# Up 2 of a two-layer feed-forward kernel: one of three token groups as seven products for eight, and every engine's order written down

## The chip, the core and the metric

The program runs on one core of one Trainium2 chip: TensorE (PE) multiplies, ScalarE (ACT), VectorE (DVE) and GpSimd (POOL) work on vectors, SyncE (SP) issues all transfers. The metric is the device time of one execution in microseconds; lower is better.

## The reference, cut to what matters

```python
attn_out = _attn_ref(**attn_kwargs)              # attention in chunks of 32, with 8 memory keys
x = attn_out.transpose(0, 2, 1, 3).reshape(B * S, H * D)       # 3072 tokens x 512
h = x @ w_in;  g = s * relu(h) ** 2 + b;  x = g @ w_out        # 512 -> 2048 -> 512
h = x @ w_in2; g = h - tanh(h);           return g @ w_out2    # 512 -> 2048 -> 512
```

All inputs are float32.

## The kernel before, in words

Five stages follow each other: attention mixed with **Up 1** (x @ w_in), **Down 1** (g @ w_out), **Up 2** (x @ w_in2 and the curve h - tanh h) and **Down 2** (g @ w_out2). In every matrix product each operand is split into a rounded "high" half and the rest, its "low" half, and the helper `three` (L123) adds high*high, low-weight*high and high-weight*low into a bank of PSUM. So a product of a 128x128 block of weights with 512 tokens is three matmuls of 128x128 by 128x512. Weights come from DRAM as 64-bit floats (`raw`) and are made float32 in four steps: `scaled` on ScalarE, `shifted`, `signed` and `filled` on VectorE. Then ScalarE copies the high half and another engine subtracts it for the low half.

The 3072 tokens are three groups (g = 0, 1, 2; NG = 3) of 1024. A product of 2 x 2 blocks can be had from seven products of sums of blocks in place of eight (P1 to P7; Strassen's scheme in Winograd's form). Down 1 and Down 2 do this before and after the change: the outer loop goes over the seven products in `ORDER` (P1, P6, P5, P7, P3, P2, P4), the inner over the three groups, each in four **entries** of 12 matmuls. So a Down stage is 7 x 3 x 4 x 12 = 1008 matmuls. For each entry `split` makes the high half (ScalarE) and the low half (VectorE) of a loaded `part` in a ring of three buffers, two entries ahead of TensorE; the third matmul of an entry is the first that reads the low half. `final` adds a finished bank to the running sums. Ready sums of g's blocks are formed at the end of each Up block by `combine` (four subtractions of 512 columns) and stored to DRAM.

Up 2 before takes the weights in eight blocks n of 1024 columns a row; each block meets the three groups with all eight products: 4 x 12 = 48 matmuls for a group, 8 x 3 x 48 = 1152 in all. Two banks are filled (24 matmuls), ScalarE takes the tanh (L794), VectorE subtracts (L795), and after two such halves GpSimd runs `combine` (L796).

The order of all engines is written by hand (`tc.manual_schedule()`) from the start to the last entry of the first product of Down 1. From there only TensorE's order is by hand (`region.enter_context(tc.manual_schedule(engines={nc.tensor.engine}))`) and a scheduler orders the others. Each engine runs its instructions in its queue's order. An instruction that waits holds what is behind it.

Of the kernel before, what the change touches and what calls it, by code (L numbers as in the profile page):

```python
# [48 lines left out]
"""  # L49

# [8 lines left out]
def tile_chunk_attention_two_ffn(  # L59
# [50 lines left out]
    def bank(k):  # L110
        return pb[:, 512 * k:512 * (k + 1)]
# [11 lines left out]
    def three(acc, whi, wlo, xhi, xlo, first, last):  # L123
        nc.tensor.matmul(acc, lhsT=whi, rhs=xhi, start=first, stop=False)  # L124
        nc.tensor.matmul(acc, lhsT=wlo, rhs=xhi, start=False, stop=False)  # L125
        nc.tensor.matmul(acc, lhsT=whi, rhs=xlo, start=False, stop=last)  # L126
# [22 lines left out]
    def to_f32(z, raw):  # L149
# [201 lines left out]
    def make_pair(raw, z_place, place, key, n, lo_pool=True):  # L351
        z = new(z_place, 1024, F32, "z")
        to_f32(z, raw)
        w = new(place, 2048, F32R, "w")
        hi, lo = w[:, 0:1024], w[:, 1024:2048]
        nc.scalar.activation(out=hi, in_=z, func=AF.Copy)
        (nc.gpsimd if lo_pool else nc.vector).tensor_tensor(out=lo, in0=z, in1=hi.bitcast(F32), op=ALU.subtract)
        wi[key, n] = tuple(t.rearrange("p (i c m) -> p i c m", i=2, c=KD) for t in (hi, lo))

# [71 lines left out]
    class Down:  # L431
# [55 lines left out]
        def sums(self, p, half, eng):  # L487

            z = lambda k: self.z[k, half]
            name = ORDER[p]  # L490

            def combo(i, x, y, op):
                t = new(self.smap[i][half], 1024, F32, f"s{i}")
                eng.tensor_tensor(out=t, in0=x, in1=y, op=op)
                self.st[i, half] = t
                return t

            if name == "P1":
                src = z("A11")
            elif name == "P6":  # L500
                s1 = combo(0, z("A21"), z("A22"), ALU.add)
                src = combo(1, s1, z("A11"), ALU.subtract)
            elif name == "P5":
                src = self.st[0, half]
            elif name == "P7":
                src = combo(0, z("A11"), z("A21"), ALU.subtract)
            elif name == "P3":
                src = self.st[1, half]
                eng.tensor_tensor(out=src, in0=z("A12"), in1=src, op=ALU.subtract)  # L509
            else:  # L510
# [46 lines left out]
        def run(self, between):  # L557
# [49 lines left out]

    def final1(name, g, ps):
        a = lambda k: sums1.at(k, g)

        def last_sum(k, x, op):
# [50 lines left out]
    region = ctx.enter_context(ExitStack())  # L662
    region.enter_context(tc.manual_schedule())
# [13 lines left out]
    for j in range(2, NBLK):  # L677
        last = j == NBLK - 1
        for t in range(16):
# [15 lines left out]
            if last and t in (4, 10):  # L695
                down1.weights(0, t // 8, nc.vector)
# [81 lines left out]

    for n in range(8):
        for g in range(NG):  # L780
            at_ = NG * n + g
            oa, ob = (
                new(C_OT[at_ % 2][h], 4 * NB, F32, ("oa", "ob")[h]).rearrange("p (s t) -> p s t", s=4)
                for h in range(2)
            )
            wh, wl = wi[2, n]
            for i in range(2):
                ps = bank2((2 * at_ + i + 1) % 4)
                for col, half in enumerate((1, 0)):
                    for c in range(KD):  # L790
                        xh, xl = x2_of(c, half, g)
                        three(ps[:, col, 0:NB], wh[:, i, c, :], wl[:, i, c, :], xh, xl, c == 0, c == KD - 1)
                r = new(C_R[i], 2 * NB, F32, "r2").rearrange("p (m t) -> p m t", m=2)
                nc.scalar.activation(out=r, in_=ps[:, :, 0:NB], func=AF.Tanh)  # L794
                nc.vector.tensor_tensor(out=oa[:, 2 * i:2 * i + 2], in0=ps[:, :, 0:NB], in1=r, op=ALU.subtract)  # L795
            combine(oa, ob, nc.gpsimd)  # L796
            nc.sync.dma_start(out=o2[g][:, n, 0:3], in_=oa[:, 1:4])
            nc.sync.dma_start(out=o2[g][:, n, 3:7], in_=ob)
            if g == 0 and n + 1 < 8:
                w2_load(n + 1)  # L800
            if g == 1 and n + 1 < 8:
                w2_make(n + 1)
            if g == 0 and 1 <= n <= 4:
                thunks.extend(down2.load_quadrant(C_RAW[1 + i]) for i in range(2))
            if g in (1, 2) and thunks:
                thunks.pop(0)()
            if n == 7 and g in (1, 2):
                down2.weights(0, g - 1)
                down2.load_to(g - 1)
    down2.run(lambda p, k: None)  # L810
# [71 lines left out]
```

## Time and profile before

| what | value |
| --- | --- |
| median of 3 runs | 1081.1 us (1080.97 to 1082.42) |
| profiled execution | 1080.99 us, span 1079.2 us |
| TensorE busy | 1060.4 us (98%), mean granted clock 0.996 |
| VectorE, ScalarE, GpSimd busy | 711.6, 486.6, 265.1 us |
| TensorE's share of the chain that ended last | 91% |

The span runs from the first to the last instruction; the profiled execution took 1.8 us more than its span. A matmul's busy time (0.39 us) overlaps the next one's, so TensorE's pace is read from starts. Idle time of an engine other than TensorE costs nothing by itself.

### The profile page before, as it was taken

To read this page: it belongs to the slowest core of one execution; us is meant where nothing else is said; L and a number is where in the kernel's file an instruction comes from. 1 tells how busy PE (TensorE), PEld (TensorE's weight loads), DVE (VectorE), ACT (ScalarE), POOL (GpSimd) and SP (SyncE) were. 2 spreads that over 40 slices of the span, in tenths; PEclk is the share of its full clock that TensorE was granted. 3 is DMA by queue.
4 is the path that set the end of the run, shared out by engine and by line. 5 is a ranking of instruction groups with operands and counts; after the bars stand their busy time and mean duration, and the time that the engine had idled before them with its cause. 6 is when DMAs were issued, how large, how long until landed. Compare 5 with 4: busy or idle time off the path is not lost.

```text
span 1079.2 us, 15211 instructions
## 1 busy us (share of the span) xinstructions
PE 1060.4 (98%) x6072; PEld 876.1 (81%) x6072; DVE 711.6 (66%) x742; ACT 486.6 (45%) x863; POOL 265.1 (25%) x164
## 2 busy tenths in 40 slices
PE   6999999999999999999999999999999999999998
PEld 5878888888888878888888888888888888888886
DVE  7997667777768895578788894332322665566654
ACT  7673665555423554455554342222222454444432
POOL 1000000000000161100100587655567941001100
PEclk8999999999999999999999999999999999999999
DMA  9764768666448856555565756545546865566751
GB/s 319 262 254 167 264 237 318 246 249 222 179 183 317 299 189 201 194 193 198 194 236 176 305 197 265 215 166 205 214 171 228 312 234 195 195 234 234 252 196 59
DMA packets 71687, 242.16 MB, mean 224 GB/s; under 512 B 5312, under 2 KB 5312, under 8 KB 61376
## 3 DMA queue, kind: packets, MB, share of 16 engines
q1 hardware_dynamic: 71616, 241.19, 62.3%
q8 instruction: 47, 0.77, 0.3%
q14 instruction: 24, 0.20, 0.0%
HBM read 146.80 MB, written 94.37 MB: 223 GB/s over the span
## 4 chain that ended last, share of the span: by engine, by line
PE 91%; DVE 5%; ACT 2%; DMA 2%; issue 1%; DVEq 0%; ACTq 0%; SPq 0%
PE pb L124 29%; PE pb L126 29%; PE pb L125 29%; PE pb L298 2%; PE pb L276 2%; PE pb L236 1%; DMA raw<-in_wi_dram 1%; ACT sm L260 1%; DVE ringhringl L535 1%; DVE ob L423 1%; DVE oa L408 0%; DVE z L145 0%; DVE w L378 0%; DVE nmx L254 0%; DMA qk<-in_qk_dram 0%
## 5 line engine op out<-in xcount | busy, mean ns | idle before, releaser
L126 PE MATMUL pb<-ringhringl,whl 128*128 128x512 f32 x560 | 218.3, 390 | 0.9 <-DVE ringhringl L535 0.9
L124 PE MATMUL pb<-ringhringl,whl 128*128 128x512 f32 x560 | 217.9, 389 | 0.0
L125 PE MATMUL pb<-ringhringl,whl 128*128 128x512 f32 x560 | 217.9, 389 | 0.0
L540 DVE TENSOR_TENSOR ringhringl<-part,ringhringl 128x1024 fp32r<-128x1024 f32 x92 | 128.5, 1397 | 84.7 <-ACT ringhringl L539 84.7
L539 ACT ACTIVATE ringhringl<-part 128x1024 fp32r<-128x1024 f32 x92 | 97.7, 1061 | 135.6 <-PE pb L126 123.2
L124 PE MATMUL pb<-xh,w 128*128 128x512 f32 (+1 forms) x392 | 153.5, 392 | 0.4 <-DVE oa L408 0.3
L126 PE MATMUL pb<-xl,w 128*128 128x512 f32 (+1 forms) x392 | 151.2, 386 | 0.6 <-DVE xl L320 0.6
L125 PE MATMUL pb<-xh,w 128*128 128x512 f32 (+1 forms) x392 | 151.1, 386 | 0.1
L795 DVE TENSOR_TENSOR oa<-pb,r 128x1024 f32<-128x1024 f32 x48 | 58.5, 1220 | 109.7 <-ACT r L794 104.6
L126 PEld LDWEIGHTS pb<-ringhringl,whl 128*128 128x128 f32 x560 | 105.1, 188 | 24.9 <-DVE ringhringl L535 2.9
L125 PEld LDWEIGHTS pb<-ringhringl,whl 128*128 128x128 f32 x560 | 105.1, 188 | 21.8
L124 PEld LDWEIGHTS pb<-ringhringl,whl 128*128 128x128 f32 x560 | 105.1, 188 | 21.7
L794 ACT ACTIVATE r<-pb 128x1024 f32<-128x1024 f32 x48 | 49.1, 1025 | 124.8 <-PE pb L126 124.3
L509 POOL TENSOR_TENSOR s<-zq,s 128x1024 f32<-128x1024 f32 x4 | 12.4, 3093 | 374.8 <-DVE whl L521 374.7
L398 ACT ACTIVATE r<-pb 128x512 f32<-128x512 f32 x96 | 55.9, 592 | 99.1 <-PE pb L126 84.8
L535 DVE SCALAR_TENSOR_TENSOR ringhringl<-part,b_c,ringhringl 128x1024 fp32r<-128x1024 f32 x48 | 76.7, 1613 | 22.2 <-ACT ringhringl L534 21.9
L408 DVE SCALAR_TENSOR_TENSOR oa<-pb,s_c,r 128x512 f32<-128x512 f32 x96 | 70.0, 745 | 29.0 <-ACT r L398 29.0
L124 PEld LDWEIGHTS pb<-xh,w 128*128 128x128 f32 x392 | 73.6, 188 | 17.5 <-DVE oa L408 1.7
L124 PE MATMUL pb<-x2hx2l,w 128*128 128x512 f32 x224 | 87.1, 389 | 0.0
L125 PE MATMUL pb<-x2hx2l,w 128*128 128x512 f32 x224 | 87.1, 389 | 0.0
L126 PE MATMUL pb<-x2hx2l,w 128*128 128x512 f32 x224 | 87.1, 389 | 0.0
L126 PEld LDWEIGHTS pb<-xl,w 128*128 128x128 f32 x392 | 73.6, 188 | 15.7 <-DVE xl L320 0.8
(108 smaller groups left out, 1811.2 us busy)
## 6 DMA issues: line engine op xcount, KB each, us to landing
o<-ob SPq DMA_DIRECT2D x48, 1024.0 KB, 4.7
part<-o SPq DMA_DIRECT2D x84, 512.0 KB, 4.6
part<-o SPq DMA_DIRECT2D x42, 1024.0 KB, 5.0
o<-oa SPq DMA_DIRECT2D x48, 768.0 KB, 3.5
raw<-in_wi_dram SPq DMA_DIRECT2D x16, 1024.0 KB, 6.4
raw<-in_wo_dram SPq DMA_DIRECT2D x16, 1024.0 KB, 7.0
qk<-in_qk_dram SPq DMA_DIRECT2D x24, 640.0 KB, 7.7
v<-in_vw_dram SPq DMA_DIRECT2D x24, 384.0 KB, 8.1
```

The costliest lines, as they stand in the source:

```text
L124: nc.tensor.matmul(acc, lhsT=whi, rhs=xhi, start=first, stop=False)
L125: nc.tensor.matmul(acc, lhsT=wlo, rhs=xhi, start=False, stop=False)
L126: nc.tensor.matmul(acc, lhsT=whi, rhs=xlo, start=False, stop=last)
L276: nc.tensor.transpose(out=bank(2 + g)[0:KE, P * r:P * (r + 1)], in_=sm[:, 4 * g + r, :], identity=ident)
L298: nc.tensor.matmul(value_bank(u)[64 * g:64 * g + 64, c0:c0 + QE], lhsT=tv[0:KE, e, 2 * r + g, :], rhs=pt[0:KE, 4 * g + r, QE * e:QE * (e + ...
L398: nc.scalar.activation(out=r, in_=up_ps[j, t], func=AF.Relu)
L408: nc.vector.scalar_tensor_tensor(out=oab[j, q][0][:, 2 * i:2 * i + 2, k, :], in0=ps2, scalar=s_c[:, 0:1], in1=r2, op0=ALU.mult, op1=ALU.mult,)
L535: nc.vector.scalar_tensor_tensor(out=xl, in0=src, scalar=self.bias, in1=xh.bitcast(F32), op0=ALU.add, op1=ALU.subtract)
L539: nc.scalar.activation(out=xh, in_=src, func=AF.Copy)
L540: nc.vector.tensor_tensor(out=xl, in0=src, in1=xh.bitcast(F32), op=ALU.subtract)
L794: nc.scalar.activation(out=r, in_=ps[:, :, 0:NB], func=AF.Tanh)
L795: nc.vector.tensor_tensor(out=oa[:, 2 * i:2 * i + 2], in0=ps[:, :, 0:NB], in1=r, op=ALU.subtract)
```

## The change

Up 2 computes the third group (g = 2) with the seven products; groups 0 and 1 stay as they were. The products are accumulated in three single banks (0, 1, 2): P1, P6, P5 and P3 follow each other in bank 0, and ScalarE copies the bank (`keep`) after P1, P6 and P5, before the next product is added to it. P7 and P4 share bank 1, P2 has bank 2. Token sums T1 to T4 are made at the end of Down 1 (`b_t3`, `b_t1`, `b_t2`) and split in block 0 of Up 2 (`t_split`), weight sums in every block (`w2_sums`, `w2_split`). All subtractions that GpSimd did go to VectorE. The order of all engines is by hand to the program's end; in the Down stages the steps that make the next product's weights stand at places given by a table `WEIGHTS`. Buffers are placed anew. Of the diff (buffer places, and what repeats, left out):

```diff
+WEIGHTS = {
+    (0, 1): [("sums", 1, 0)], (0, 2): [("high", 1, 0)], (0, 4): [("low", 1, 0)],
...
-    C_RAW, C_Z, C_W = ("E0", "E8", "E10"), "Z5", ("E1", "E2")
+    C_RAW, C_Z, C_W = "E0", "Z5", ("E1", "E2")
...
+    D_RAW = ("E0", "E1")
...
-        def weights(self, p, half, eng=nc.gpsimd):
-            self.sums(p, half, eng)
+        def weights(self, p, half):
+            self.sums(p, half)
             self.high(p, half)
-            self.low(p, half, eng)
...
-                elif p + 1 < 7 and k in (5, 9):
-                    self.weights(p + 1, (k - 5) // 4)
+                for step, q, half in WEIGHTS.get((p, k), ()):
+                    getattr(self, step)(q, half)
                 between(p, k)
...
-        if p == 0 and k == 4 * NG - 1:
-            region.close()
-            region.enter_context(tc.manual_schedule(engines={nc.tensor.engine}))
...
+        if p == 6 and k < 3:
+            (lambda: (w2_load(0), b_t3()), b_t1, b_t2)[k]()
+        if p == 6 and 4 <= k < 4 + len(w2_steps):
+            w2_steps[k - 4](0)
...
+    def end_out(n, g):
+        oa, ob = outs.pop((n, g))
+        combine(oa, ob, nc.vector)
+        nc.sync.dma_start(out=o2[g][:, n, 0:3], in_=oa[:, 1:4])
+        nc.sync.dma_start(out=o2[g][:, n, 3:7], in_=ob)
...
+        strassen("P1")
+        copy(1)
+        strassen("P7")
+        strassen("P6")
+        copy(2)
+        yield
+        strassen("P5")
+        copy(3)
+        strassen("P2")
+        add(2, 3, 1)
+        strassen("P3")
+        add(1, 1, 2)
+        strassen("P4")
+        yield
+        curve(0, bank(0))
+        curve(1, oa[:, 1])
+        curve(2, oa[:, 2])
+        add(3, 2, 1)
+        curve(3, oa[:, 3])
+        yield
+        end_out(n, g)
...
     for n in range(8):
...
+        for col in range(2):
+            plain_column(n, 1, 0, col)
+        if last:
+            quads[3]()
...
+        else:
+            w2_steps[0](n + 1)
+        plain_end(n, 1, 0)
+        if last:
+            quads[4]()
+            fetch(6, 1)
...
+            down2.load_to(0)
+        else:
+            for step in w2_steps[1:]:
+                step(n + 1)
...
+        plain_column(n, 1, 1, 0)
+        group = quad(n)
+        next(group)
+        plain_column(n, 1, 1, 1)
+        plain_end(n, 1, 1)
+        next(group)
+        end_out(n, 1)
+    down2.load_to(1)
+    down2.split(0)
+    down2.split(1)
+    next(group)
```

`w2_steps` holds six steps for the next block's weights: `scaled` with `shifted`; `signed`; `filled`; high half (ScalarE); low half; the four weight sums of 256 columns. `curve` is a tanh on ScalarE and a subtraction on VectorE, `add` one sum on VectorE. In a block TensorE's order is: both columns of half (0,0), of (0,1) and of (1,0), 24 matmuls each; a column of (1,1), 12; P1, P7, P6, 6 each; the other column of (1,1), 12; P5, P2, P3, P4, 6 each: 138 matmuls.

ScalarE in Up 2, block 1, from the conversion of block 2's weights on. L144 is `scaled`, L877 the tanh of a plain half, L749 the high half of the next block's weights, L900 the copies of bank 0 (`keep`), L909 the curves.

```order
L144 ACTIVATE z<-raw 128x1024
L877 ACTIVATE r_5382<-pb 128x1024
L749 ACTIVATE w<-z 128x1024
L900 ACTIVATE keep<-pb 128x512 x2
L877 ACTIVATE r_5444<-pb 128x1024
L900 ACTIVATE keep_5411<-pb 128x512
```

The rows of the kernel before at such a place (L794 the tanh, L356 the high half, L131 `scaled`):

```order
L794 ACTIVATE r_5248<-pb 128x1024
L356 ACTIVATE w<-z 128x1024
L131 ACTIVATE z<-raw 128x1024
L794 ACTIVATE r_5283<-pb 128x1024
L516 ACTIVATE whl<-zq 128x1024
```

The copies of bank 0 are new, and two of them stand behind the high half of the next block's weights, which waits for VectorE's `filled` of the same block; TensorE's P6 waits for the first copy, P5 for the second.

VectorE in Down 1, product P7, second group: before the change, L616 finishes Q, L624 adds to U, L540 is the low half of a split, L621 the low half of Q for Up 2.

```order
L616 TENSOR_TENSOR q<-sumV,pb 128x1024
L624 TENSOR_TENSOR sumU<-sumU,pb 128x1024
L540 TENSOR_TENSOR ringhringl<-part,ringhringl 128x1024
L621 TENSOR_TENSOR x2hx2l<-q,x2hx2l 128x1024
L540 TENSOR_TENSOR ringhringl<-part,ringhringl 128x1024
```

And with the change (L630, L639, L646 and L547 are the same four):

```order
L630 TENSOR_TENSOR q<-sumV,pb 128x1024
L639 TENSOR_TENSOR x2hx2l<-q,x2hx2l 128x1024
L646 TENSOR_TENSOR sumU<-sumU,pb 128x1024
L547 TENSOR_TENSOR ringhringl<-part,ringhringl 128x1024 x2
```

Q's low half, which needs ScalarE's high half of the same Q, has moved ahead of the next split.

VectorE at the border of Up 2 and Down 2, with the change, from the last `combine` (L430) of group 1 on. L547 is a split of Down 2, L910 a curve's subtraction, L903 an `add`, L501 the weight sums of P6.

```order
L430 TENSOR_TENSOR ob<-ob,oa 128x512
L547 TENSOR_TENSOR ringhringl<-part,ringhringl 128x1024 x2
L910 TENSOR_TENSOR oa<-pb,r_6779 128x512
L910 TENSOR_TENSOR oa<-oa,r_6779 128x512
L910 TENSOR_TENSOR oa<-oa,r_6784 128x512
L903 TENSOR_TENSOR oa<-keep,pb 128x512
L910 TENSOR_TENSOR oa<-oa,r_6784 128x512
L547 TENSOR_TENSOR ringhringl<-part,ringhringl 128x1024
L430 TENSOR_TENSOR ob<-oa 128x512
L430 TENSOR_TENSOR ob<-oa,ob 128x512
L430 TENSOR_TENSOR ob<-oa 128x512
L430 TENSOR_TENSOR ob<-ob,oa 128x512
```

Behind them stand a split (L547), the two sums (L501), two splits and one weight conversion. Before the change VectorE's rows at this border are:

```order
L540 TENSOR_TENSOR ringhringl<-part,ringhringl 128x1024
L795 TENSOR_TENSOR oa<-pb,r_6602 128x1024
L795 TENSOR_TENSOR oa<-pb,r_6642 128x1024
L795 TENSOR_TENSOR oa<-pb,r_6669 128x1024
L540 TENSOR_TENSOR ringl<-part,ringh 128x1024
L540 TENSOR_TENSOR ringhringl<-part,ringhringl 128x1024 x2
```

The sums of g and of the weights, which were GpSimd's, now stand between the splits, and the first two splits stand behind the last `combine` of group 1.

## Rows read from the trace of the kernel before

**Rows 1.** Page, part 1: each engine's busy time and share of the span.

```profile
PE 1060.4 (98%) x6072; PEld 876.1 (81%) x6072; DVE 711.6 (66%) x742; ACT 486.6 (45%) x863; POOL 265.1 (25%) x164
```

**Rows 2.** Busy time by stretch: Down 1, Up 2, Down 2; (x) counts starts.

```profile
353.55:584.38 230.83, 229.89 (x1009) 188.83 (x1008) 178.86 (x134) 122.37 (x115) 45.26 (x16) 1.00 0.60 203
584.38:845.50 261.12, 261.12 (x1153) 216.29 (x1152) 119.05 (x91) 74.24 (x73) 167.47 (x106) 1.00 0.58 223
845.50:1074.04 228.54, 228.54 (x1009) 188.96 (x1007) 137.97 (x102) 100.09 (x96) 49.67 (x19) 1.00 0.61 212
```

**Rows 3.** Timeline of VectorE in Down 1: start, us, line, tiles, count.

```profile
379.20 1.28 DVE L535 SCALAR_TENSOR_TENSOR ringhringl<-part,b_c,ringhringl 128x1024 fp32r<-128x1024 f32 x1 [0.97 <-ACT ringhringl L534]
...
381.53 19.18 DVE L535 SCALAR_TENSOR_TENSOR ringhringl<-part,b_c,ringhringl 128x1024 fp32r<-128x1024 f32 x7
```

**Rows 4.** Timeline of GpSimd in the same stretch of Down 1.

```profile
381.76 3.31 POOL L509 TENSOR_TENSOR s<-zq,s 128x1024 f32<-128x1024 f32 x1 [8.21 <-DVE whl L521]
...
395.16 3.27 POOL L494 TENSOR_TENSOR s<-zq 128x1024 f32<-128x1024 f32 x1
```

**Rows 5.** Timeline of Down 2: TensorE, VectorE and ScalarE around a bank's last product.

```profile
1030.29 0.39 PE L126 MATMUL pb<-ringhringl,whl 128*128 128x512 f32 x1
...
1030.72 1.06 ACT L539 ACTIVATE ringhringl<-part 128x1024 fp32r<-128x1024 f32 x1 [1.89 <-PE pb L126]
...
1030.72 1.22 DVE L753 TENSOR_TENSOR o<-sumX,pb 128x1024 f32<-128x1024 f32 x1 [0.63 <-PE pb L126]
```

**Rows 6.** Timeline of ScalarE in Up 2: a curve.

```profile
682.50 1.03 ACT L794 ACTIVATE r<-pb 128x1024 f32<-128x1024 f32 x1 [4.41 <-PE pb L126]
```

**Rows 7.** Timeline of VectorE in Up 2: the subtraction behind that curve.

```profile
683.56 1.22 DVE L795 TENSOR_TENSOR oa<-pb,r 128x1024 f32<-128x1024 f32 x1 [4.16 <-ACT r L794]
```

**Rows 8.** Timeline of VectorE in Up 1: one weight conversion.

```profile
171.00 0.68 DVE L135 TENSOR_SCALAR zq<-zq 128x1024 int32<-128x1024 int32 x1
...
171.72 1.22 DVE L139 SCALAR_TENSOR_TENSOR zq<-raw,zq 128x1024 int32<-128x1024 int32 x1
...
172.97 1.22 DVE L145 SCALAR_TENSOR_TENSOR zq<-raw,zq 128x1024 int32<-128x1024 int32 x1
```

**Rows 9.** Timeline of VectorE in Up 1: four sums and what follows.

```profile
204.08 0.68 DVE L423 TENSOR_TENSOR ob<-oa 128x512 f32<-128x512 f32 x1
...
206.61 0.75 DVE L408 SCALAR_TENSOR_TENSOR oa<-pb,s_c,r 128x512 f32<-128x512 f32 x1
```

**Rows 10.** Timeline of VectorE in Up 2: the end of a conversion.

```profile
640.90 1.21 DVE L145 SCALAR_TENSOR_TENSOR zq<-raw,zq 128x1024 int32<-128x1024 int32 x1
```

**Rows 11.** Timeline of ScalarE in Up 2: `scaled`, then a copy that waits for VectorE.

```profile
629.60 1.14 ACT L131 ACTIVATE zq<-raw 128x1024 f32<-128x1024 f32 x1
...
642.20 1.06 ACT L516 ACTIVATE whl<-zq 128x1024 fp32r<-128x1024 f32 x1 [10.55 <-DVE zq L145]
...
643.17 1.92 ACT L794 ACTIVATE r<-pb 128x1024 f32<-128x1024 f32 x2
```

**Rows 12.** Page, part 5: reads of one 512-column bank by ScalarE.

```profile
L398 ACT ACTIVATE r<-pb 128x512 f32<-128x512 f32 x96 | 55.9, 592 | 99.1 <-PE pb L126 84.8
```

**Rows 13.** Timeline of VectorE in Down 1: the end of a P7 product.

```profile
475.61 1.22 DVE L616 TENSOR_TENSOR q<-sumV,pb 128x1024 f32<-128x1024 f32 x1 [0.40 <-PE pb L126]
...
476.75 1.22 DVE L624 TENSOR_TENSOR sumU<-sumU,pb 128x1024 f32<-128x1024 f32 x1
...
477.88 1.22 DVE L540 TENSOR_TENSOR ringhringl<-part,ringhringl 128x1024 fp32r<-128x1024 f32 x1
...
479.02 1.22 DVE L621 TENSOR_TENSOR x2hx2l<-q,x2hx2l 128x1024 fp32r<-128x1024 f32 x1
```

**Rows 14.** Timeline of GpSimd at the border of Up 2 and Down 2.

```profile
847.89 2.40 POOL L509 TENSOR_TENSOR s<-zq,s 128x1024 f32<-128x1024 f32 x1
```

**Rows 15.** Loads of part (835 to 900 us) and raw (584 to 840 us).

```profile
DMA to landing us min/median/max: 4.7/6.4/7.6
...
DMA to landing us min/median/max: 4.8/6.0/7.4
```

More of the change, by code (lines that the diff above doesn't have):

```diff
@@ L121, in tile_chunk_attention_two_ffn, with three @@
     b_c = const.tile([P, 1], F32, name="b_c")
[L123 to L126, printed above, removed]
+    def three(acc, whi, wlo, xhi, xlo, first, last, more=False):
+        nc.tensor.matmul(acc, lhsT=whi, rhs=xhi, start=first, stop=False, skip_group_check=more)
+        nc.tensor.matmul(acc, lhsT=wlo, rhs=xhi, start=False, stop=False, skip_group_check=more)
+        nc.tensor.matmul(acc, lhsT=whi, rhs=xlo, start=False, stop=last, skip_group_check=more)
     def scaled(z, raw):
@@ L349, in load_raw @@
         return raw
[L351 to L358, printed above, removed]
     raws, w1_z, w1_w = {}, {}, {}
@@ L695, in tile_chunk_attention_two_ffn @@
             if last and t in (4, 10):
-                down1.weights(0, t // 8, nc.vector)
+                down1.weights(0, t // 8)
             if last and t in (4, 10, 11):
@@ L777, in tile_chunk_attention_two_ffn @@
     )
-    for n in range(8):
[L780 to L809, printed above, removed]
@@ new lines, in tile_chunk_attention_two_ffn, with fetch @@
+    quads = {}
+    def fetch(k, place=0):
+        quads[k] = down2.load_quadrant(D_RAW[place])
+    group = None
+    for n in range(8):
+        last = n == 7
+        before = group
+        begin_out(n, 0)
+        for col in range(2):
+            plain_column(n, 0, 0, col)
+        if before is not None:
+            next(before)
+        if n in (2, 4, 6):
+            quads[n // 2 - 1]()
+        if not last:
+            w2_load(n + 1)
+        else:
+            fetch(3, 0)
+            fetch(4, 1)
+        plain_end(n, 0, 0)
+        if before is not None:
+            next(before)
+        if n == 0:
+            t_split("T3")
+            t_split("T2")
+        w2_split(n)
+        for col in range(2):
+            plain_column(n, 0, 1, col)
+        plain_end(n, 0, 1)
+        end_out(n, 0)
+        if n == 0:
+            t_split("T1")
+            t_split("T4")
+        begin_out(n, 1)
+        for col in range(2):
+            plain_column(n, 1, 0, col)
+        if last:
+            quads[3]()
+            down2.sums(0, 0)
+            down2.high(0, 0)
+            down2.low(0, 0)
+            fetch(5, 0)
+        else:
[4 more added lines that the diff above has]
+            fetch(6, 1)
+            down2.sums(0, 1)
+            down2.high(0, 1)
+            down2.low(0, 1)
+            down2.load_to(0)
+        else:
+            for step in w2_steps[1:]:
+                step(n + 1)
+            if n in (1, 3, 5):
+                fetch(n // 2)
+        plain_column(n, 1, 1, 0)
[5 more added lines that the diff above has]
+        end_out(n, 1)
@@ L813, in _up_layout, with between2 @@
+    down2.load_to(1)
+    down2.split(0)
+    down2.split(1)
+    next(group)
+    def between2(p, k):
+        if p == 0 and k == 0:
+            next(group)
+        if p == 0 and k == 3:
+            quads[5]()
+            fetch(7, 0)
+        if p == 1 and k == 6:
+            quads[6]()
+        if p == 1 and k == 9:
+            quads[7]()
+    down2.run(between2)
 def _up_layout(w):
```

173 lines of the change are left out of this document (140 added, 33 removed).

## The prediction

> **What bounds it now.** The first view is the page's busy shares: TensorE is busy for 98% of the span [rows 1]. So time comes only from matmuls left out and from places where TensorE stops. The windows of the three stages show where these are [rows 2]. Up 2 starts 1152 matmuls in 261.12 us and is busy for all of it, so one matmul costs 261.12/1152 = 0.2267 us at a granted clock of 1.00: 2.72 us an entry or column of 12, 1.36 a product of 6, 5.44 a half of 24. Down 2 takes 228.54 us for 1008 matmuls, which is 1008 x 0.2267 = 228.5: no stop. Down 1 takes 230.83 us, 2.3 to 2.4 more. The timelines say where that goes: VectorE's split takes 1.28 us alone and 19.18/7 = 2.74 us [rows 3] while GpSimd sums weights between 381.76 and 398.4 us [rows 4]. Nothing else stops TensorE from Down 1 on, so a vector engine matters only where its chain is longer than the matmuls ahead of the one that waits for it.
>
> The pieces of such chains. ScalarE or VectorE starts 0.43 us after the start of a bank's last matmul [rows 5], so 0.43 - 0.23 = 0.20 us after that matmul's slot. A tanh takes 1.03 us [rows 6], and VectorE's subtraction starts 0.03 us behind it [rows 7]. Behind one another, VectorE's 1024-column instructions start 1.14 us apart [rows 13], a conversion's `shifted` and `signed` take 0.72 and 1.25 us to the next start, `filled` 1.22 us [rows 8], four 512-column sums 2.53 us [rows 9]. A ScalarE copy starts 0.09 us after VectorE's `filled` has ended [rows 10, 11], the next instruction 0.97 us later, `scaled` takes 1.14 us [rows 11], and reading one bank 0.59 us [rows 12]. From there to a waiting matmul I take 0.08 us, an estimate by the 0.03 and 0.09 above.
>
> **The change part by part.**
>
> *Matmuls.* Up 2 has 138 a block in place of 144: 8 x 6 x 0.2267 = **-10.9**.
>
> *GpSimd leaves Down 1's head.* Without its sums beside VectorE the splits should take 1.28 us again: **-2.4**, the whole loss of that stage.
>
> *P6's wait in Up 2.* P6 needs ScalarE's copy of bank 0 after P1. In ScalarE's queue that copy stands behind the high half of the next block's weights, which waits for VectorE's `filled`, and `filled` stands behind the subtraction of half (1,0). From that half's end: 0.20 + tanh 1.03 + 0.03 + subtraction 1.14 + `signed` 1.25 + `filled` 1.22 + 0.09 + high half 0.97 + copy 0.59 + 0.08 = 6.60 us. Meanwhile TensorE has a column, P1 and P7, 24 matmuls or 5.44 us. That is 1.16 us of stop, in blocks 1 to 6: **+7.0**. What is queued behind the high half is the first copy, and TensorE itself waits for it; P5's copy follows freely. Block 7 makes no next weights of this stage, and its high halves wait on nothing of VectorE: 0. The rest of the seven products (VectorE's `add`s, the curves one block later) has at least the 24 matmuls of a half to hide in: 0; if that cover were gone, a 512-column sum is 0.68 us [rows 9].
>
> *Block 0* also splits the token sums. From the end of half (0,1): 0.20 + 1.03 + 0.03, then VectorE without a gap: subtraction 1.14, `combine` 2.53, two low halves 2.28, `shifted` 0.72, subtraction of half (1,0) 1.14, `signed` 1.25, `filled` 1.22; then 0.09 + 0.97 + 0.59 + 0.08. Together 13.26 us against 24 + 24 matmuls, 10.88: **+2.4**.
>
> *Down 1, product P7.* Q's low half now stands before the splits. Before, Q, U, split and Q's low half started 1.14 us apart with nothing waiting between [rows 13]. Now, from a bank's end: 0.20 + Q 1.22 + 0.09 + ScalarE's copy 1.06 + 0.03 + Q's low half 1.14 + U 1.14 + split 1.23 + 0.08 = 6.19 us, and the third matmul of the entry that needs this split comes after two entries and two matmuls, 5.89: 0.30 for each group, **+0.9**. If ScalarE's copy is hidden, it is 0.
>
> *Down 1, product P4, entry 10.* ScalarE and VectorE wait for each other twice on the way from g = 0's sum to the split of entry 10: a sum, four ScalarE instructions, six of VectorE (the conversion's `signed` and `filled` among them), three of ScalarE, a low half. With the pieces above that ends 17.7 us after the bank, and six entries and two matmuls are 16.8: **+1.0**.
>
> *Down 2's head.* Call the end of Up 2's last product T. VectorE's last `combine` of group 1 stands behind an `add` that waits for P2, whose bank is ready at T - 2.72 + 0.20 = T - 2.52. `add` 0.60 and `combine` 2.53 bring it to T + 0.61, split 0 (1.23) to T + 1.84; the third matmul of entry 0 is due at T + 0.45, so at least 1.5 us of stop. Split 0's load was issued by SP behind the load of weights that waits for the conversion before it, about T - 6.5. It lands 4.7 to 7.6 us later [rows 15], then copy, 0.03 and split: 1.5 to 3.1 us of stop, of which I take 2.0 (near the median, 6.4, the `combine` and the load both bind). Then VectorE has 14.5 us in one queue from T + 0.7 on: two splits, four curves and an `add` with their wait for P4's tanh, a split, `combine`, a split, two weight sums of 1024 columns, the split of entry 4. That ends near T + 15.2, and entry 4's third matmul is due at T + 10.88 + 0.45: 3.9 to 4.6 us late in all. ScalarE's high half of the sum, its `scaled` and the next conversion on VectorE follow, with 3.1 us for the conversion's three steps by [rows 8]; entries 6 and 8 are then 6.4 to 6.8 late, with a late load up to 9. I take **+7.0**, range +6.5 to +9. Before, the sums at this place were GpSimd's [rows 14] and no entry waited [rows 2].
>
> The Trainium skill's page "SBUF — State Buffer", section "The DMA setup-cost knee", gives a transfer about 2 us and its bytes at 436 GB/s, an estimate of 4.4 us for a megabyte. The trace differs: 4.7 us at the least and 6.4 in the median for such a load [rows 15]. By the page's figure the load would never bind and the stop at entry 0 were 1.5 us, the sum 1085.5.
>
> *Sum*, from the profiled execution of 1080.99 us (its median of runs is 1081.1, the same within 0.1): 1081.0 - 10.9 - 2.4 + 7.0 + 2.4 + 0.9 + 1.0 + 7.0 = **1086.0 us**.
>
> **Rivals.**
>
> *A, the copy is not held up: faster.* The wait of P6 decides at 5.44 us: if the chain is 1.2 us shorter, as it is if the scheduler of the queues lets ScalarE take the copy of bank 0 ahead of the waiting high half, the +7.0 and +2.4 go: 1086.0 - 9.4 = **1076.6**. For it: ScalarE is busy 74 of 261 us in Up 2 [rows 2], so it has room. Against: at 642.20 us its copy sat 10.55 us waiting for VectorE's `filled`, and two tanhs started only behind it, at 643.17 [rows 11].
>
> The Trainium skill's page "TensorE: Matmul & The Clock Gate", in the specification table at its head, calls the queues of ScalarE and VectorE strictly first in, first out. By that A cannot come about, and the trace's tanhs agree.
>
> *B, Down 2's head is hidden*: 1086.0 - 7.0 = **1079.0**, about the time of before. It needs the first splits ready before T, so the `combine` of group 1 ahead of the `add` that waits. For it: the ring has three buffers, and the first load is issued in block 7. Against: the order of VectorE's rows.
>
> *C, the weights come late in Up 2.* In blocks 2, 4 and 6 the buffer of raw weights first serves a conversion for Down 2, so that the load of the next block's weights starts only some 8 us into the block. Landing at +7.4 it is just in time (15.4 us, then `scaled` 1.14 before 16.5); each us over that adds one to each of three blocks. For it: the longest landing of such loads is 7.4, and 7.6 for parts [rows 15]. With +2.4 to +5.4, and Down 2's parts 1.5 late, it gives **1090 to 1092**. Against: the median is 6.0.
>
> **How the numbers follow.** Forecast 0.58, A 0.13, B 0.17, C 0.12. A measurement tells about 0.2%, 2.2 us, from no change: 1078.9 to 1083.3. The forecast's own bounds: the P7 and P4 terms 0 to 1.9, Down 2's head 6.5 to 9, the 0.20 and 0.08 of each P6 chain +-0.2 x 7: 1082.7 to 1089.4; nearly all of it is slower, 0.55, with 0.03 the same. A is faster; B lies at the lower edge of the same, 0.14 the same and 0.03 faster; C is slower. So faster 0.16, same 0.17, slower 0.67. The range goes from 1078.5, which leaves out A, to 1092.0, the end of C.
>
> **What would show it.** In Up 2's window: 1104 matmul starts, and 250.2 + 9.4 us, with the stops on the first matmul of P6, put down to ScalarE's copy of bank 0, 1.2 us in each of blocks 1 to 6, 2.4 in block 0. In Down 1: splits of 1.28 us at the head, and 1.9 us lost in P7 and P4 on L547. In Down 2: about 7 us before entry 10, with VectorE busy without a gap. The prediction is wrong if P6 starts behind P7 at once, if the first splits of Down 2 end before its first entry, or if VectorE, without GpSimd beside it, runs faster in Up 2 than the rows used here.

## The result and the profile after

The changed kernel takes 1091.72 us (median of 4, 1090.34 to 1092.93), the kernel before 1081.18: a ratio of 1.0095, 95% interval 1.0077 to 1.0112. It is slower, inside the range, but by 10.5 us where 4.9 were forecast. The profiled execution took 1092.42 us, span 1090.6.

First the page's shares of the kernel after, then the windows of its three stages, which answer to [rows 1, 2]; behind each engine's busy time stands the number of starts, behind the last one TensorE's granted clock.

```profile
PE 1055.8 (97%) x6024; PEld 867.5 (80%) x6024; DVE 813.3 (75%) x969; ACT 510.4 (47%) x914; POOL 2.7 (0%) x24
354.14:584.33 230.19, 229.70 (x1010) 188.88 (x1009) 171.89 (x149) 115.86 (x110) 0.00 (x0) 1.00 0.58 195
584.33:846.06 261.73, 253.96 (x1105) 207.64 (x1103) 202.57 (x262) 96.75 (x118) 0.00 (x0) 0.99 0.56 211
846.06:1085.50 239.44, 232.03 (x1009) 189.52 (x1008) 163.11 (x144) 107.74 (x106) 0.00 (x0) 0.99 0.64 225
```

GpSimd has nothing left in these stages, VectorE went from 711.6 to 813.3 us over the whole span, and TensorE is no longer busy for the whole of Up 2 and Down 2. Down 1 takes 230.19 us, 0.64 less than before; Up 2 takes 261.73 us where 1104 matmuls without a stop are 250.2; Down 2 takes 239.44 where 1008 are 228.5. Down 1 began 0.59 us later, though nothing ahead of it had changed; in the profiles of this study that start lies between 353.5 and 355.2. So 0.59 - 0.64 + 0.61 + 10.90 = 11.46, which is the whole difference of the two profiled executions (11.43). All that the 48 matmuls gave, and more, stands in stops.

**Down 1.** VectorE's split at the place of [rows 3], then the end of the one long stop, entry 10 of P4: VectorE's split and TensorE's third matmul.

```profile
380.54 1.28 DVE L542 SCALAR_TENSOR_TENSOR ringhringl<-part,b_c,ringhringl 128x1024 fp32r<-128x1024 f32 x1
...
577.88 1.23 DVE L547 TENSOR_TENSOR ringhringl<-part,ringhringl 128x1024 fp32r<-128x1024 f32 x1 [0.67 <-ACT ringhringl L546]
...
579.16 0.50 PE L139 MATMUL pb<-ringhringl,whl 128*128 128x512 f32 x1 [0.30 <-DVE ringhringl L547]
```

Splits take 1.28 us, the 2.35 us of before are gone, and 1.6 us of new stops (three of 0.3 in P7, one of 0.6 in P4) came instead. These losses are read from the starts of matmuls, and each holds 0.10 to 0.12 us by which the second matmul behind a stop starts late.

**Up 2.** Blocks 0 and 1 around P6: VectorE's `filled`, ScalarE's high half of the next weights and copy, then P6's first matmuls. Idle time before an instruction and its releaser stand in brackets.

```profile
605.39 1.23 DVE L158 SCALAR_TENSOR_TENSOR z<-raw,z 128x1024 int32<-128x1024 int32 x1
...
606.65 1.06 ACT L749 ACTIVATE w<-z 128x1024 fp32r<-128x1024 f32 x1 [4.78 <-DVE z L158]
607.62 0.58 ACT L900 ACTIVATE keep<-pb 128x512 f32<-128x512 f32 x1
...
605.86 0.39 PE L139 MATMUL pb<-t,shl 128*128 128x512 f32 x1
608.25 0.51 PE L137 MATMUL pb<-t,shl 128*128 128x512 f32 x1 [2.00 <-ACT keep L900]
608.59 0.60 PE L138 MATMUL pb<-t,shl 128*128 128x512 f32 x1
608.98 0.63 PE L139 MATMUL pb<-t,shl 128*128 128x512 f32 x1
609.41 0.63 PE L137 MATMUL pb<-t,shl 128*128 128x512 f32 x1
...
641.06 0.39 PE L139 MATMUL pb<-t,shl 128*128 128x512 f32 x1
642.35 0.50 PE L137 MATMUL pb<-t,shl 128*128 128x512 f32 x1 [0.91 <-ACT keep L900]
642.69 0.39 PE L138 MATMUL pb<-t,shl 128*128 128x512 f32 x1
```

The chain is the one that was forecast: `filled`, high half, copy, P6, one behind the other. In block 1, P6 starts 1.29 us after the matmul ahead of it, 1.06 more than the pitch of 0.23, and its second matmul 0.34 after the first, 0.11 more: 1.17 us of loss. The sum had a stop of 1.16 us and nothing for the second matmul. In block 0 the stop is 2.16 us, and nine matmuls behind it start up to 0.43 us apart. Their window, with the granted clock of 0.56 third from the end, is mostly at the lower level, 1.2 GHz:

```profile
608.25:612.10 3.85, 3.85 (x10) 3.06 (x11) 2.41 (x5) 0.60 (x1) 0.00 (x0) 0.56 0.00 0
```

Block 6 loses 1.51 us: VectorE's subtraction there waited 0.69 us for a store that still read the buffer.

```profile
799.84 1.23 DVE L878 TENSOR_TENSOR oa<-pb,r 128x1024 f32<-128x1024 f32 x1 [0.69 <-DMA o<-oa]
```

**Down 2's head.** The end of Up 2 (T) is at 846.06. First SyncE's issues (loads of parts and stores of group 1), then ScalarE's high halves, then TensorE's matmuls behind the stops.

```profile
839.64 0.43 SPq L811 DMA_DIRECT2D part<-o  x1
...
846.86 0.32 SPq L864 DMA_DIRECT2D o<-ob  x1
847.29 5.63 SPq L811 DMA_DIRECT2D part<-o  x4
...
847.27 2.01 ACT L546 ACTIVATE ringhringl<-part 128x1024 fp32r<-128x1024 f32 x2 [4.49 <-DMA part<-o]
...
856.52 2.00 ACT L546 ACTIVATE ringhringl<-part 128x1024 fp32r<-128x1024 f32 x2 [2.74 <-DMA part<-o]
...
848.38 0.50 PE L137 MATMUL pb<-ringhringl,whl 128*128 128x512 f32 x1 [2.16 <-ACT ringhringl L546]
848.71 0.40 PE L138 MATMUL pb<-ringhringl,whl 128*128 128x512 f32 x1
...
849.64 0.50 PE L139 MATMUL pb<-ringhringl,whl 128*128 128x512 f32 x1 [0.53 <-DVE ringhringl L547]
...
857.63 0.68 PE L137 MATMUL pb<-ringhringl,whl 128*128 128x512 f32 x1 [2.70 <-ACT ringhringl L546]
...
858.89 0.80 PE L139 MATMUL pb<-ringhringl,whl 128*128 128x512 f32 x1 [0.15 <-DVE ringhringl L547]
...
873.30 0.50 PE L139 MATMUL pb<-ringhringl,whl 128*128 128x512 f32 x1 [1.47 <-DVE ringhringl L547]
```

Part 0 was issued at 839.64, T - 6.4, and ScalarE could read it at 847.27, 7.6 us later; entry 0 lost 3.2 us. Part 1 was issued only at 847.29, behind the store of group 1 that waits for the `combine`, and was there at 856.52, 9.2 us later. Entry 2 lost 4.8 us on it, of which 1.3 are again slow matmuls (granted clock 0.66 from 857 to 862). Entries 4, 6 and 8 lost 0.7, 1.7 and 0.3 on VectorE's splits. The five loads of parts issued between 820 and 866 us, four of them one right behind the other, landed after (minimum, median, maximum):

```profile
DMA to landing us min/median/max: 7.6/11.5/12.8
```

### The profile page after: what moved, and what is told of

The parts are those of the page before. It is cut to its first block, busy times and chain, and to the rows that moved or that the text cites. A ratio compares the mean times of both kernels' runs of the same rounds, so it can differ in the third digit from the quotient of the medians.

```text
span 1090.6 us, 15131 instructions
## 1 busy us (share of the span) xinstructions
PE 1055.8 (97%) x6024; PEld 867.5 (80%) x6024; DVE 813.3 (75%) x969; ACT 510.4 (47%) x914; POOL 2.7 (0%) x24
## 4 chain that ended last, share of the span: by engine, by line
PE 80%; DVE 9%; ACT 4%; DMA 4%; issue 2%; SPq 0%; ACTq 0%; DVEq 0%
PE pb L137 26%; PE pb L139 25%; PE pb L138 25%; PE pb L314 2%; PE pb L292 1%; DVE z L158 1%; PE pb L252 1%; DVE ob L430 1%; DVE z L152 1%; ACT sm L276 1%; DMA raw<-in_wo_dram 1%; DMA o<-oa 1%; DMA part<-o 1%; ACT w L749 1%; ACT r L877 1%
## 5 line engine op out<-in xcount | busy, mean ns | idle before, releaser
L137 PE MATMUL pb<-ringhringl,whl 128*128 128x512 f32 x672 | 262.4, 390 | 4.9 <-ACT ringhringl L546 4.9
L139 PE MATMUL pb<-ringhringl,whl 128*128 128x512 f32 x672 | 263.0, 391 | 3.0 <-DVE ringhringl L547 2.8
L138 PE MATMUL pb<-ringhringl,whl 128*128 128x512 f32 x672 | 262.0, 390 | 0.0
L547 DVE TENSOR_TENSOR ringhringl<-part,ringhringl 128x1024 fp32r<-128x1024 f32 x120 | 146.4, 1223 | 78.5 <-ACT ringhringl L546 78.5
L546 ACT ACTIVATE ringhringl<-part 128x1024 fp32r<-128x1024 f32 x120 | 126.3, 1059 | 150.2 <-PE pb L139 133.2
L139 PEld LDWEIGHTS pb<-ringhringl,whl 128*128 128x128 f32 x672 | 126.4, 188 | 33.4 <-DVE ringhringl L547 6.6
L137 PEld LDWEIGHTS pb<-ringhringl,whl 128*128 128x128 f32 x672 | 126.4, 188 | 31.5 <-ACT ringhringl L546 5.7
L138 PEld LDWEIGHTS pb<-ringhringl,whl 128*128 128x128 f32 x672 | 126.5, 188 | 26.4
L137 PEld LDWEIGHTS pb<-xh,w 128*128 128x128 f32 x392 | 73.6, 188 | 17.7 <-DVE oa L415 1.8
L276 ACT ACTIVATE sm<-sm,nmx 128x96 f32<-128x96 f32 x192 | 69.1, 363 | 37.8 <-DVE nmx L270 37.8
L138 PEld LDWEIGHTS pb<-xh,w 128*128 128x128 f32 x392 | 73.7, 188 | 14.9 <-DVE w L385 0.9
L542 DVE SCALAR_TENSOR_TENSOR ringhringl<-part,b_c,ringhringl 128x1024 fp32r<-128x1024 f32 x48 | 61.3, 1283 | 25.2 <-ACT ringhringl L541 24.8
L139 PE MATMUL pb<-x2hx2l,w 128*128 128x512 f32 x192 | 74.7, 389 | 0.0
L138 PE MATMUL pb<-x2hx2l,w 128*128 128x512 f32 x192 | 74.7, 389 | 0.0
L137 PE MATMUL pb<-x2hx2l,w 128*128 128x512 f32 x192 | 74.7, 389 | 0.0
L541 ACT ACTIVATE ringhringl<-part,b_c 128x1024 fp32r<-128x1024 f32 x48 | 54.9, 1147 | 36.3 <-PE pb L139 33.5
```

The source lines that it names most:

```text
L276: nc.scalar.activation(out=sm[:, h, :], in_=sm[:, h, :], func=AF.Exp, bias=nmx[:, h:h + 1], scale=1.0, accum_out=sums[:, h:h + 1],)
L541: nc.scalar.activation(out=xh, in_=src, func=AF.Identity, bias=self.bias)
L542: nc.vector.scalar_tensor_tensor(out=xl, in0=src, scalar=self.bias, in1=xh.bitcast(F32), op0=ALU.add, op1=ALU.subtract)
L546: nc.scalar.activation(out=xh, in_=src, func=AF.Copy)
L547: nc.vector.tensor_tensor(out=xl, in0=src, in1=xh.bitcast(F32), op=ALU.subtract)
```

## The experiments

Medians, each beside runs of the kernel before, whose medians were 1080.9 to 1081.2:

| run | median, us | ratio to before, 95% interval | Down 1, Up 2, Down 2 of its profile, us |
| --- | --- | --- | --- |
| after | 1091.72 | 1.0077 to 1.0112 | 230.2, 261.7, 239.4 |
| e1_copies_first | 1080.96 | 0.9985 to 1.0003 | 230.2, 250.5, 239.6 |
| e2_sums_split_later | 1089.94 | 1.0064 to 1.0092 | 230.2, 259.3, 238.6 |
| e3_parts_earlier | 1087.14 | 1.0037 to 1.0062 | 230.2, 261.5, 235.0 |
| e4_parts_splits_earlier | 1084.76 | 1.0018 to 1.0043 | 230.2, 259.8, 233.3 |
| e5_orders | 1079.10 | 0.9973 to 0.9990 | 230.2, 251.4, 236.0 |
| e6_orders_down1 | 1077.60 | 0.9955 to 0.9980 | 228.5, 252.6, 235.9 |
| e7_gpsimd_at_head | 1094.42 | 1.0108 to 1.0135 | 230.2, 261.8, 242.0 |
| e8_before_sums_vector | 1078.69 | 0.9969 to 0.9987 | 228.5, then 489.7 as before |
| e9_loads_ahead | 1072.41 | 0.9908 to 0.9935 | 228.5, 252.8, 229.7 |
| e10_add_first | 1071.06 | 0.9891 to 0.9924 | 228.5, 250.4, 231.3 |

**P6's wait (e1).**

```diff
-            for step in w2_steps[1:]:
+            for step in w2_steps[1:3]:
                 step(n + 1)
...
         next(group)
+        if not last:
+            for step in w2_steps[3:]:
+                step(n + 1)
         plain_column(n, 1, 1, 1)
```

> Only the place of three steps in Up 2 is moved: the high half, low half and sums of the next block's weights stand behind the copies of bank 0 after P1 and P6, in place of ahead of them. Theory (the copy after P1 is held in ScalarE's queue by the high half that waits for VectorE's conversion): the copy is ready 0.20 + 0.51 + 0.08 = 0.8 us after P1's end, P6 starts 1.36 us after it, so all seven stops of Up 2 go, with the slow matmuls behind the first one: Up 2 from 261.7 to about 250.3 us, the whole from 1091.7 to 1080.5 (1079.5 to 1082). Rival (VectorE's work itself is too long for a block, so that the wait only moves to the next block's first matmul or to P7): Up 2 stays above 258 us, the whole above 1088.

The windows of Up 2 and Down 2:

```profile
584.00:834.50 250.50, 250.50 (x1105) 207.01 (x1103) 201.82 (x262) 96.68 (x118) 0.00 (x0) 1.00 0.58 220
834.50:1074.12 239.62, 232.57 (x1009) 189.75 (x1008) 163.13 (x144) 107.79 (x106) 0.00 (x0) 0.99 0.65 224
```

Up 2 has no stop left, 1104 matmuls in 250.50 us at a granted clock of 1.00, and the whole falls by 10.8 us. VectorE's busy time is the same 202 us, so its load was never the limit: the order was. The edit moves three steps at once, the high half on ScalarE and the low half and the sums on VectorE; that the high half is the one that counted is read from the rows above, where the copy starts right behind it. Down 2 did not move.

**Block 0 and the clock (e2).** The lines `if n == 0: t_split("T1"); t_split("T4")` move from behind `end_out(n, 0)` to behind `next(group)`.

> Only block 0 of Up 2 changes: the splits of the token sums T1 and T4 stand behind the copies after P1 and P6, so that 2.28 us of VectorE's work leave the chain ahead of P6. Theory (a stop of 2.2 us lets TensorE's granted clock fall, one of 1.1 us does not): block 0 stops for 1.1 us like blocks 1 to 5, at 2.4 GHz; 1.1 us of stop and 1.7 us of slow matmuls go, the whole falls by 2.8 to 1088.9. Rival (the slow matmuls come at this place whatever the length of the stop, from the program's own activity): 1.1 us only, 1090.6, and the granted clock around 608 to 612 us stays near 0.6.

```profile
606.74 0.39 PE L139 MATMUL pb<-t,shl 128*128 128x512 f32 x1
608.03 0.50 PE L137 MATMUL pb<-t,shl 128*128 128x512 f32 x1 [0.91 <-ACT keep L900]
608.37 0.39 PE L138 MATMUL pb<-t,shl 128*128 128x512 f32 x1
608.60 0.40 PE L139 MATMUL pb<-t,shl 128*128 128x512 f32 x1
```

Block 0 now stops like block 1, and the matmuls behind the stop keep their 0.23 us. Up 2 is 2.4 us shorter. The median is 1.8 us lower and lies between the two forecasts, so it does not decide; the pitch behind the stop favours the theory. But another run limits it: e4 has the same stop of 2.16 us at the same place, and its matmuls stayed fast. The window 605 to 613 us of its profile:

```profile
605.00:613.00 8.00, 6.00 (x27) 4.63 (x26) 4.42 (x7) 2.50 (x4) 0.00 (x0) 1.00 0.00 0
```

Three of the four profiles with that stop show the slow matmuls (the kernel after, e3, e7), one does not. P6's stops of 1.06 us kept the clock in every profile. So did a stop of 2.32 us at entry 0 of Down 2 in the kernel after (granted clock 1.00 from 846 to 857 us) and one of 2.07 us in e9; in e1 a stop of 2.36 us at that entry 0 was followed by slow matmuls some 2 us later. Why one stop of two microseconds lowered the clock and another did not stays open.

**Down 2's loads and splits (e3, e4).** e3 moves the two loads; e4 has the four lines with `split` besides:

```diff
         if last:
+            down2.load_to(0)
             quads[3]()
...
-            down2.load_to(0)
...
+        if last:
+            down2.load_to(1)
+            down2.split(0)
+            down2.split(1)
         plain_column(n, 1, 1, 1)
...
-    down2.load_to(1)
-    down2.split(0)
-    down2.split(1)
     next(group)
```

> Only the issue of Down 2's first two loads of parts is moved: part 0 ahead of the loads of two weight quadrants, part 1 ahead of group 1's last stores. VectorE's and ScalarE's orders stay. Theory (of the 10.9 us that Down 2 loses, the part above VectorE's queue comes from loads that are issued behind waiting instructions): the first split waits for the combine alone, 1.6 us at entry 0 in place of 3.2, the 4.8 us at entry 2 shrink to under 1.5, VectorE's queue then binds at entries 4 to 8: Down 2 loses 6.5 to 7, the whole falls by 4 to 1087.7. Rival (the DMA engines are full there, over 0.9 busy, so that the same bytes land at the same time): Down 2 still loses over 9.5, the whole above 1090.

> The loads as in the run with earlier parts, and the first two splits of Down 2 stand behind the copy after P6 of the last block, ahead of the adds and the combine of group 1. Theory: entries 0 and 1 do not stop, VectorE's queue from T + 0.7 us on is 2.3 us shorter, entry 4 is 1.6 us late and entries 6 to 8 4 to 4.5 us in all: Down 2 loses 4.5, the whole falls by 6.4 to 1085.3. Rival (what counts is the length of VectorE's queue until entry 8, whatever the order in it, or the loads of parts 2 to 5): Down 2 loses 6.5 or more, no better than with earlier parts alone.

In e3 T is 846.64. VectorE's last row of `combine` and the splits behind it, then TensorE's waiting matmul:

```profile
846.72 0.68 DVE L430 TENSOR_TENSOR ob<-ob,oa 128x512 f32<-128x512 f32 x1
847.33 2.35 DVE L547 TENSOR_TENSOR ringhringl<-part,ringhringl 128x1024 fp32r<-128x1024 f32 x2
...
848.60 0.50 PE L139 MATMUL pb<-ringhringl,whl 128*128 128x512 f32 x1 [1.35 <-DVE ringhringl L547]
```

And the window 846 to 860 us of the kernel after, then of e3; the last two numbers are the DMA engines' busy share and the GB/s.

```profile
846.00:860.00 14.00, 8.47 (x30) 5.66 (x30) 8.63 (x12) 6.85 (x9) 0.00 (x0) 0.92 1.03 373
```

```profile
846.00:860.00 14.00, 11.49 (x48) 8.35 (x47) 12.98 (x18) 4.71 (x7) 0.00 (x0) 1.00 1.02 362
```

Now the split starts as soon as the `combine` is done. Entry 0 loses 1.6 us in place of 3.2, entry 2 loses 0.9 in place of 4.8, and Down 2 6.5 in all: what the sum's own chain of VectorE gives without a late load. So the loads were worth 4.4 us of Down 2, and the rival falls: the DMA engines are as full as in the kernel after, and still the time of issue counted. In e4 Down 2 loses 4.8, with 4.5 expected; nearly all that is left (five losses of 0.3 to 1.7 us) stands on the low half of a split, VectorE's.

**GpSimd again (e7).** On top of e4, `combine` of group 2 in block 7 and the sums of P6's weights in Down 2 go to `nc.gpsimd`.

> As the run with earlier parts and splits, but GpSimd does group 2's last combine and the sums of P6's weights in Down 2, as in the kernel before. Theory (VectorE's queue at Down 2's head is what stops TensorE, and the move of GpSimd's sums into it costs that): VectorE has 5 us less to do ahead of entry 4, Down 2 loses under 2 us in place of 4.6, the whole 1081.7 (1080.5 to 1083). Rival (beside GpSimd VectorE's splits take about 2.7 us each, as at the head of Down 1 before): Down 2 loses 4 us or more, the whole 1084 or above.

GpSimd's sums and VectorE's splits there:

```profile
856.66 3.36 POOL L501 TENSOR_TENSOR s<-zq 128x1024 f32<-128x1024 f32 x1
...
853.28 7.81 DVE L547 TENSOR_TENSOR ringhringl<-part,ringhringl 128x1024 fp32r<-128x1024 f32 x3
```

The theory fell. Three splits take 7.81 us, 2.60 each in place of 1.22, GpSimd's sum 3.36, and Down 2 loses 13.5 us. The queue of VectorE costs, but with splits this tight GpSimd beside it costs more. The kernel before had the same sums on GpSimd at this place [rows 14] and lost nothing in Down 2 [rows 2], though its splits beside GpSimd's work took 1.64 to 2.47 us. One of them:

```profile
852.23 2.47 DVE L540 TENSOR_TENSOR ringhringl<-part,ringhringl 128x1024 fp32r<-128x1024 f32 x1 [0.87 <-ACT ringhringl L539]
```

VectorE had nothing but splits there from 849 to 866 us and sat idle before each; in e7 the curves and an `add` stood ahead of three splits. That this was the room its splits had is read from the rows, and no run tried it.

**GpSimd in Down 1 (e8).** In the kernel before, `self.weights(p + 1, (k - 5) // 4)` gets `nc.gpsimd if self.turn else nc.vector` as its engine.

> The kernel before, with the weight sums and low halves of Down 1 on VectorE in place of GpSimd and nothing else changed by hand. Theory (the 2.3 us that Down 1 lost at its head came from GpSimd's sums beside VectorE's splits): Down 1 takes 228.6 us, the whole 1078.8 (1078 to 1079.8). Rival (the sums now stand in VectorE's queue ahead of splits and stop TensorE there): 1081 or above.

```profile
353.59:582.07 228.48, 228.48 (x1010) 189.19 (x1009) 173.90 (x148) 122.13 (x115) 4.85 (x2) 1.00 0.62 206
```

Down 1 takes 228.48 us, no loss, and the whole 1078.69: 2.5 us less for one argument (the sums now stand on VectorE between the splits, which take 1.28 us each).

**Putting it together (e5, e6, e9, e10).** e5 joins e1 and e4 and spreads what stood at Down 2's head:

```diff
         yield
-        end_out(n, g)
+        combine(oa, outs[n, g][1], nc.vector, 1)
+        nc.sync.dma_start(out=o2[g][:, n, 3:7], in_=outs.pop((n, g))[1])
...
+    down2.split(2)
     next(group)
+    late = {
+        3: [("sums", 1, 0)], 4: [("high", 1, 0)], 6: [("low", 1, 0)],
+        7: [("sums", 1, 1)], 8: [("high", 1, 1)], 9: [("low", 1, 1)],
+    }
...
-        if p == 0 and k == 0:
+        if p == 0 and k in (1, 2):
             next(group)
```

The store of `oa` stands behind the last curve, the two halves of `combine` in entries 1 and 2, and `late` is the place of P6's weights in Down 2.

> The order of Up 2 as in the run with the copies first, the loads and first splits of Down 2 as in the run with earlier parts and splits, and besides at Down 2's head: the third split stands ahead of the four curves, the combine of group 2 two entries later, the sums and halves of P6's weights two entries later. Same instructions, other places. Theory (what Down 2 still lost, 4.6 us, is the length of VectorE's queue ahead of each split): Up 2 takes 250.3 us, Down 2 loses under 1.5 us, the whole comes to 1070.5 (1069.5 to 1073). Rival (with VectorE's queue short, the loads of parts 2 to 5 bind, with the DMA engines over 0.9 busy): Down 2 loses 3 to 5 us, the whole 1073 to 1076.

The forecast failed by 8.6 us, and for most of it the rows show my own edit as the cause: SyncE's store of `oa`, which waits for the last curve, now stood ahead of the load of part 2 and those behind it, and ScalarE's split waited for part 2. Down 2 lost 7.5 us, and Up 2 1.1.

```profile
842.69 0.32 SPq L932 DMA_DIRECT2D o<-oa  x1
843.10 6.19 SPq L812 DMA_DIRECT2D part<-o  x5
...
850.17 2.00 ACT L546 ACTIVATE ringhringl<-part 128x1024 fp32r<-128x1024 f32 x2 [7.28 <-DMA part<-o]
...
851.28 0.76 PE L137 MATMUL pb<-ringhringl,whl 128*128 128x512 f32 x1 [4.52 <-ACT ringhringl L546]
```

It is the mechanism of part 1 once more: 4.7 us of stop, and slow matmuls behind it. e6 moves `tt("U", "U", ALU.add)` ahead of Q's low half, and the first weights' high half, low half and sums at entries 8 to 10 in place of 7 to 9.

> As the run with all orders, and in Down 1 the addition to U stands ahead of Q's low half in P7, and the high half, low half and sums of Up 2's first weights one entry later in P4. Theory (the stops of P7 and P4 come from a split that stands behind an instruction waiting for ScalarE): the three stops of 0.3 us and the one of 0.6 us go, 1.6 us less than the run with all orders: 1069.0. Rival (the stops come from ScalarE's load in these products, whatever VectorE's order): within 0.5 us of that run.

Down 1 fell from 230.20 to 228.48 us, 1.7 where 1.6 were expected; the whole is 1.5 us under e5's, and missed 1069.0 because that forecast stood on e5's. Up 2 lost 2.3 us here, 1.6 of them at P3 of the last block. P3 waits for the copy after P5, which stood in ScalarE's queue behind two splits, and these waited for part 0:

```profile
829.41 2.01 ACT L546 ACTIVATE ringhringl<-part 128x1024 fp32r<-128x1024 f32 x2 [2.65 <-DMA part<-o]
...
832.87 0.50 PE L137 MATMUL pb<-x2hx2l,shl 128*128 128x512 f32 x1 [1.31 <-ACT keep L902]
```

e9 puts `split(0)` and `split(1)` behind `copy(3)`, `load_to(2)` ahead of group 1's stores, and `load_to(3)` ahead of group 2's.

> As the run with all orders and Down 1, but the first two splits of Down 2 stand behind the copy after P5, the load of part 2 is issued there, ahead of group 1's stores, and that of part 3 ahead of group 2's first store (in the run before this one parts 2 to 4 were issued behind that store, which waits for the last curve, and entry 4 waited 4.6 us for part 2). Theory (that wait, and the copy after P5 that stood behind two splits waiting for part 0, are places in a queue): entry 4 and the products P3 and P5 no longer wait, Down 2 loses under 1.5 us, the whole falls from 1077.6 to 1069.6 (1068.5 to 1072). Rival (the DMA engines are full at this border, and the parts land late wherever they are issued): over 1074.

It missed its range by 0.4 us. Down 2 lost 1.2, but P4 had a new wait, for an `add` that I had let slip behind the two splits:

```profile
830.97 0.39 PE L139 MATMUL pb<-x2hx2l,shl 128*128 128x512 f32 x1
833.27 0.50 PE L137 MATMUL pb<-t,w 128*128 128x512 f32 x1 [1.91 <-DVE oa L905]
```

e10 puts `strassen("P2")` and `add(2, 3, 1)` ahead of the splits.

> As the run with loads ahead, but the first add of the last block's group 2 stands ahead of the first two splits of Down 2 on VectorE (in that run P4 waited 2.1 us, since it adds to the bank that this add reads, and the add stood behind the splits). Theory: that stop goes and no other comes, the whole falls by 2.2 from 1072.4 to 1070.2 (1069.4 to 1071.4). Rival (the splits, now later, or the combine behind them stop entry 0 or 2 instead): over 1071.8.

```profile
353.93:582.40 228.47, 228.47 (x1009) 189.25 (x1008) 172.24 (x149) 115.89 (x110) 0.00 (x0) 1.00 0.59 196
582.40:832.79 250.39, 250.39 (x1105) 206.98 (x1103) 201.71 (x261) 98.69 (x120) 0.00 (x0) 1.00 0.57 224
832.79:1064.05 231.26, 229.88 (x1009) 188.80 (x1008) 162.89 (x146) 105.88 (x104) 0.00 (x0) 1.00 0.67 228
```

Up 2's stop is gone; 2.7 us remain in Down 2, of which 0.9 are entry 0's first matmul, which waits for the second `add`, now behind the splits: the rival's mechanism, at less than its price. This version is 0.9% faster than the kernel before, and 20.7 us faster than the change as it was made, with the same instructions.

## Why the prediction was right in sign and wrong in size

Of the 6.5 us by which the stages came out above the sum, Down 2 gives 3.9, Up 2 2.1, the later start of Down 1 0.6 and Down 1 itself -0.1.

*Matmuls, -10.9.* Right: Up 2 starts 1104, and e1 runs them in 250.5 us.

*GpSimd out of Down 1's head, -2.4.* Right: splits of 1.28 us, and e8 gives 2.5 us with that alone.

*P7 +0.9 and P4 +1.0.* Measured 1.0 and 0.6; e6 takes both away. That P7 came so near is in part luck: 0.3 of the 1.0 are second matmuls, for which the sum had nothing. P4's chain of 17.7 us was given without its single terms, so which of them was too long stays open.

*P6's wait, +7.0.* The mechanism and its place were right, and e1 removes it. The stop was 1.06 us a block where the sum had 1.16; that the loss, 1.17, meets it to 0.01 is luck, since 0.11 of it is the second matmul. Rival A fell: the copy started at 607.62, right behind the high half of 606.65, though P1's last matmul had started at 604.50. The Trainium skill's page "TensorE: Matmul & The Clock Gate", in the specification table at its head, has ScalarE's queue strictly first in, first out; the trace agrees, the copy starting 0.97 us after the high half.

*Block 0, +2.4.* The stop was 2.16 us. The term was short of the nine matmuls at the lower clock behind it, 1.6 us, and the 0.11 us that a second matmul loses behind a stop. With block 6's 0.34 more, Up 2 lost 11.5 us against 9.4.

*Down 2's head, +7.0: the step that failed, with 10.9.* The working said "Split 0's load was issued by SP behind the load of weights that waits for the conversion before it, about T - 6.5. It lands 4.7 to 7.6 us later [rows 15]", and took 2.0 us near the median. The issue was right to 0.1 us; the landing was at the upper end, 7.6, and the stop 3.2. Worse, the part-1 load was not followed at all: SP's queue holds it behind group 1's last store, which waits for the `combine`, so it could not be issued before T + 1.2 or read before T + 10.5, when entry 2, already late by 3.2, was due at T + 8.7. That and the slow matmuls made 4.8 us. The third step, VectorE's queue, was right: with the loads in time e3 loses 6.5, the lower bound of the term. The clause "with a late load up to 9" saw the direction and stopped short, since [rows 15] reach to 900 us and so take in stretches in which the DMA engines were less busy: a share of 1.00 from 846 to 860 us, 0.76 to 883, 0.54 to 900. Between 820 and 866 us the loads of parts took 11.5 us in the median in the kernel after, and in the kernel before:

```profile
DMA to landing us min/median/max: 4.9/7.1/8.4
```

The Trainium skill's page "SBUF — State Buffer", section "The DMA setup-cost knee", from which 4.4 us were estimated, was further off; no load of a part in that stretch of the kernel after took less than 7.6.

*Rivals.* B fell: the head was not hidden. Its condition would not have been enough: in e4 the first splits are ready before T, and Down 2 still loses 4.8 us. The measured 1091.7 lies in C's range of 1090 to 1092, but by luck. Of C, the part on Down 2's loads came true, with 3.9 us in place of 1.5; the one on Up 2's weights did not, and only block 6 lost 0.34 us, to a store. C's own terms reach from 1089.9 to 1092.9 and not to 1092, and the forecast's lower bound, with Down 2's 6.5 in it, is 1082.2 and not 1082.7; neither changes the account.

## What to carry to other kernels

A stop can be priced from rows of the kernel before to some tenths of a microsecond (1.06 us where 1.16 were summed, 2.16 where 2.4) if the chain is written out instruction by instruction; what the sum lacked was a queue that it had not walked, SyncE's, where one store that waits for a sum held four loads. Follow the second and third load as far as the first. When an order is written by hand, look at each instruction that waits and ask what stands behind it: moves of that kind turned 1% slower into 0.9% faster without changing the work.

## What the hardware showed beyond the expectation

After a stop that kept the clock the second matmul starts 0.31 to 0.35 us after the first in place of 0.23, so a stop costs some 0.1 us more than its wait. P6's stop of 2.16 us was followed by matmuls 0.43 us apart in three of four profiles, the one of 1.06 us in none. Beside GpSimd's 1024-column sums (3.2 to 3.4 us) VectorE's splits take 2.6 us in e7, more than twice the 1.22 us that they take alone.
